# Linear attention, a mixture of experts and an MLP on one core: the mask table's source, the order of the input loads, and the last slot's routing

## The chip, the cores and the metric

The kernel runs on one core of one Trainium2 chip. A core has five engines that run their own instruction streams: PE (matrix products), DVE and POOL (elementwise work), ACT (activation functions, copies with a scale) and SP (which here only issues DMAs). DMAs are issued by SP, ACT and POOL and are carried out by 16 DMA engines. The metric is the device time of one launch in microseconds (us), the median of several runs.

## The reference

Three stages follow each other. First a linear attention with decay, for 2 batches, 8 heads, 768 positions and 64 dimensions per head:

```python
for b in range(nb):                                   # blocks of 64 positions
    intra = (q_b @ k_b.T * Dmask) @ v_b               # Dmask[i,j] = lam**(i-j) for i >= j, else 0
    inter = (q_b * lam**(pos+1)) @ kv_state
    out[b] = intra + inter
    kv_state = lam**block * kv_state + (k_b * lam**(block-1-pos)).T @ v_b
```

Its output, 1536 tokens of 512 numbers, goes through a mixture of 8 experts in which each token takes the one expert whose embedding is nearest to it: `out = gate * (relu(x @ w1[e]) @ w2[e])`, with 512 by 1024 and 1024 by 512 weights per expert. The result goes through an MLP with 2048 hidden units, `elu(x @ w_in) @ w_out`. The MLP's weights arrive as 64-bit floats and are converted on the chip.

## The kernel before

The kernel works in 12 **slots** of 128 tokens: slot s is block s // 2 (128 positions) of batch s % 2. A slot's input is 1 MB, loaded by two DMAs of 512 KB: `load_a` brings the queries and keys (lines 323 to 331), `load_b` the keys again in the other layout and the values. Everything is issued in an order written out by hand (`manual_schedule`), so each engine's stream is what the code says.

Attention per slot: `stage_a` forms the scores (PE, `st`, L344), `mask` multiplies them by the decay table `Dm` (DVE, `stm`, L352), `queries` and `keys` scale q and k (POOL, `qd` and `kd`), `stage_b` adds the state's part and the part inside the block (PE, `xp`, L380 and L387) and copies the sum to SBUF (ACT, `xs`), `products` and `add` update the state `S` (PE `kr` L407, POOL L412, DVE L422). `stage_c` is a generator whose steps are handed out one at a time: transpose and router logits (PE `tm`), logits to SBUF (DVE `lg`), the row's norm (ACT `sq`, `yr`; DVE `nrm`, `rs`), the token rows as a high half (ACT L449) and a low half (DVE L452) of 16-bit numbers, and the DMA `rows<-row` that writes them to DRAM (SP, L455). Between these steps `self.step()` hands out one piece of weight preparation: ACT L151 writes a weight's high half, DVE L155 the low half, and the freed buffer's next load (`raw<-w`, 1 MB, SP, L129) is issued.

The decay table. `powers` (L266) forms the powers of lam, one head in each of the partitions 0 to 7 (`zs`, 8 rows of 256 numbers: zeros, then 128 powers), and writes them to DRAM (`Z`, 8 KB, on ACT's queue). `masks` reads `Dm` (128 partitions by 8 heads by 128) back from `Z` by one DMA of 512 KB whose partition p starts p numbers further on, and `scales` reads `L`, the powers per head pair, by two DMAs of 128 KB; POOL then multiplies `L` by lam (L486).

Inputs. Slots 0 to 5 are loaded at the start. `IN_AT = {2: 6, 3: 7, 4: 8, 5: 9, 8: 10, 9: 11}` says at which slot's turn which further slot is loaded; slots 4 and 5 live in two of the six weight buffers of the attention phase (`IN_W`), the others in four input buffers.

DMA counters. Each DMA issued from SP or ACT signals one of eight counters, DMAHW0 to DMAHW7, taken in turn in the program's order over both queues; before a counter is taken again, the issuing engine waits until the DMA that had it eight issues before has landed. The names in the rows of order below are these counters.

The end of the attention. Slots 9, 10 and 11 don't go through DRAM for expert 0: `first_gather` fetches expert 0's rows among slots 0 to 8 by two indirect DMAs on POOL (`g<-rows,idx`, 128 and 96 rows, L762), and `dispatch` sums them and the rows of slots 9 to 11 into `px` by products on PE (L725 and L729 for the gathered rows, L712 for the slots), using one-hot matrices `oh` from `places`. `route` ranks the tokens of a slot within their expert (PE `kr<-M`, L631 and L634, then DVE). The program waits, before the first gather, for the index tile `idx` (DVE L677) and for the DMAs that wrote the rows of slots 0 to 8.

Lines 536 to 566 order all this by hand; `go(a, b, ...)` takes one step of each generator named. Then `moe_mlp` runs the experts (PE `ph` L942, `py` L981) and the MLP (`pf` L1023, `po` L1063).

Of the kernel before, what the change touches and what calls it, by code (L numbers as in the profile page):

```python
# [9 lines left out]
F32 = mybir.dt.float32  # L10
# [35 lines left out]

IN_W = (4, 5)
IN_AT = {2: 6, 3: 7, 4: 8, 5: 9, 8: 10, 9: 11}
ATT_LOADS = (2, 4, 5, 6, 7)
# [15 lines left out]
class K:  # L65
    def __init__(self, ctx, tc, A, out, dbg=None):
        self.ctx, self.tc, self.nc, self.A, self.out = ctx, tc, tc.nc, A, out
        self.dbg = dbg or {}
        self.raws = {}
        self.wts = {}  # L70
        self.next_load = 0
        self.ring = []
# [30 lines left out]
    def piece_scale(self, i):  # L103
        if i < 4 * E:
            return (S_W1, S_W2)[(i % 4) // 2]
        return (S_WI, S_WO)[(i - 4 * E) % 2]

    def w_free(self):

        n = len(self.ring)  # L110
        if len(self.wp) == 1:
            return n < WA
        return n < WA + WB or self.used.get(self.ring[n - WA - WB], self.group) < self.group

    def w_tile(self, i):
        self.ring.append(i)
        return self.wp[(len(self.ring) - 1) % (WA + WB) >= WA].tile([P, 2, 4, 512], F16, name=f"w{i}", tag="w")

# [147 lines left out]
    def powers(self, a1, ps):  # L266

        nc = self.nc

        Z = self.dp.tile([H, 256], F32, name="Z")  # L270
        zs = a1.tile([H, 256], F32, name="zs")
        nc.vector.memset(zs, 0.0)
        pw = a1.tile([P, H], F32, name="pw")
        nc.gpsimd.tensor_tensor(out=pw, in0=self.lam8, in1=self.pcol.to_broadcast([P, H]), op=ALU.pow)
        self.kdec = pw
        nc.tensor.matmul(ps[0:H, 0:P], pw, self.id32, start=True, stop=True, skip_group_check=True)
        nc.vector.tensor_copy(zs[:, 127:255], ps[0:H, 0:P])
        nc.scalar.dma_start(Z[:, :], zs)
        return Z[:, :]

    def masks(self, a1, zt):
        nc = self.nc
        self.Dm = a1.tile([P, H, P], F32, name="Dm")
        hank = bass.AP(tensor=zt.tensor, offset=zt.offset, ap=[[1, P], [256, H], [1, P]])
        nc.sync.dma_start(self.Dm, hank)

    def scales(self, a1, zt):

        nc = self.nc
        self.L = a1.tile([P, NP, P], F32, name="L")  # L290
        for hh in range(2):
            src = bass.AP(tensor=zt.tensor, offset=zt.offset + hh * 256 + 127, ap=[[0, 64], [512, NP], [1, P]])
            nc.sync.dma_start(self.L[hh * 64 : hh * 64 + 64], src)


    def attention(self, ctx):
# [171 lines left out]
        zt = self.powers(a1, ps_r)
        self.masks(a1, zt)
        load_a(2)  # L470
        load_b(2)
        self.scales(a1, zt)
        nc.scalar.dma_start(self.c32[:, 128:], A["c32"][:, 128:])
        for s in range(3, 6):
            load_a(s)
            load_b(s)
# [3 lines left out]
        for k in range(KD):  # L480
# [4 lines left out]
        keys(1)  # L485
        nc.gpsimd.tensor_tensor(  # L486
            out=self.L, in0=self.L, in1=self.lam4[:, :, None].to_broadcast([P, NP, P]), op=ALU.mult
        )
        stage_a(0)
# [8 lines left out]
        for s in range(1, FIRST + 1):  # L498
# [51 lines left out]
        stage_a(11)  # L550
        go(c8)
        self.step()
        go(c8, c9, r8, r8, c9, r8, c9, r8)
        stage_b(10)
        fg = self.first_gather(a1, ps_r)
        go(fg, c9, c9)
# [3 lines left out]
        go(t9, t9, t9, t9, c10, c10, c10)  # L560
        stage_b(11)
        go(c9, t10, t10, fg, c10, t10, fg, c10, t10)
        go(r10, r10, put, c10)
        go(c11, c11, t11, c11, t11, c11, t11, c11, t11)
        go(put, r11, c10, put, r11, put, c11, c11, put)
        go(r10, r10, r11, r11)
# [123 lines left out]
    def dispatch(self, a1, ps_s):  # L690
# [26 lines left out]
        places(FIRST, NS - 1)  # L717
        yield
        pts = [ps_s.tile([P, 2, 2, 256], F32, name=f"px{i}", tag="st") for i in range(2)]
        g0, g1 = self.G.pop((0, 0)), self.G.pop((0, 1))  # L720
        at = lambda k: pts[k // 4][:, k // 2 % 2, k % 2]
        for i in range(2):
# [9 lines left out]
            for s in range(FIRST, NS - 1):  # L732
                products(s, ks)
            if i == 0:
                yield
        yield
        places(NS - 1, NS)
        yield
        for b in range(2):
# [535 lines left out]
def layout(q, k, v, lam, moe_expert_emb, moe_tau, moe_w1, moe_w2, moe2_w_in, moe2_w_out):  # L1275
# [22 lines left out]
    wo = moe2_w_out.view(np.int64).reshape(4, 4, P, 512).transpose(0, 2, 1, 3)  # L1298
    c32, c16 = constants()
    i1 = np.tile(np.arange(1, CAP + 1, dtype=np.float32), (P, 1))  # L1300
    return dict(i1=i1, qkv=qkv, small=small, w1=w1, w2=w2, wi=wi, wo=wo, c32=c32, c16=c16)

# [16 lines left out]
```

## Time and profile before

| | us |
|---|---|
| median of 3 runs | 508.62 |
| lowest, highest run | 508.29, 512.58 |
| the profiled execution's own time | 509.62 |
| span from its first to its last instruction | 507.8 |

The profile is of one execution, so all places in time below are in us from the start of its span. Engines are busy: PE 471.9 (93%), DVE 347.1 (68%), ACT 224.4 (44%), POOL 77.1 (15%). A row of the timeline has the start, the duration, the engine, the line, the operation, output<-inputs, the shape, the count, and in brackets how long the engine stood idle before it and what ended that. SPq and ACTq are DMA issues. A row of the windows view has a stretch, its length, the busy time (and number) of PE, PE's weight loads, DVE, ACT and POOL, then the granted TensorE clock as a share of 2.4 GHz, the busy share of the DMA engines and the GB/s. "DMA to landing" is the time from a DMA's issue until it has landed.

The attention takes the first 80 us, the hand-over to expert 0 the next 12, the experts run to about 250 us and the MLP to the end.

### The profile page before, as it was taken

Reading aid. Unit: us, or ns where it says so; the run is one execution under the profiler, and the core shown is the slowest. Engines: PE = TensorE matmul, PEld = TensorE weight load, DVE = VectorE, ACT = ScalarE, POOL = GpSimd, SP = SyncE. Lnnn points to the kernel's source line nnn. Section 1 sums busy time; section 2 is a strip of 40 time slices with the busy share of each in tenths; the row PEclk is TensorE's granted clock in tenths of the full one; section 3 lists DMA queues with packets and bytes.
Section 4 is the critical chain, followed back from the end, with each engine's and each line's share of the span. In section 5 each row is a group of like instructions: output and inputs, shape, how many; then the busy total and the mean of one; then the engine's idle time right before and its main releaser. Section 6 shows DMA issues by size and latency. Waiting matters only on the chain.

```text
span 507.8 us, 9088 instructions
## 1 busy us (share of the span) xinstructions
PE 471.9 (93%) x3671; PEld 330.6 (65%) x3671; DVE 347.1 (68%) x625; ACT 224.4 (44%) x374; POOL 77.1 (15%) x67
## 2 busy tenths in 40 slices
PE   7788885998999999979999999999999999999992
PEld 6677775997999999979844444444444444445561
DVE  2467795466999988996878797978845335435352
ACT  1255344174686676423265354534333342433441
POOL 4456431351011310000000000000000002001111
PEclk9899898998999999999999999999999999999998
DMA  7999933267999999893622222000000001101101
GB/s 223 363 411 420 416 109 137 86 155 251 336 346 231 368 378 302 335 342 121 214 85 83 84 83 84 1 1 1 0 1 0 1 0 43 41 1 42 43 28 61
DMA packets 28335, 79.07 MB, mean 156 GB/s; under 512 B 13280, under 2 KB 15360, under 8 KB 22144
## 3 DMA queue, kind: packets, MB, share of 16 engines
q1 hardware_dynamic: 25848, 71.42, 41.4%
q0 software_dynamic: 2112, 6.82, 4.1%
q8 instruction: 31, 0.51, 0.4%
q10 hardware_dynamic: 328, 0.19, 0.1%
q14 instruction: 16, 0.13, 0.1%
HBM read 68.57 MB, written 7.10 MB: 149 GB/s over the span
## 4 chain that ended last, share of the span: by engine, by line
PE 77%; DVE 5%; DMA 3%; SPq 1%; issue 1%; ACT 1%; POOL 0%; POOLq 0%; DVEq 0%
PE pf L1023 25%; PE po L1063 24%; PE ph L942 14%; PE py L981 13%; DMA x<-g 2%; DVE w L155 1%; SPq L921 1%; DVE stm L352 1%; DMA g<-rows,idx 1%; PE px L712 1%; DMA out<-o,idx 1%; DVE S L422 0%; DVE row L452 0%; PE st L344 0%; PE pt L926 0%
## 5 line engine op out<-in xcount | busy, mean ns | idle before, releaser
L1023 PE MATMUL pf<-yT,w 128*128 128x512 f16 (+2 forms) x672 | 133.2, 349 | 0.0
L1063 PE MATMUL po<-w,g 128*128 128x512 f16 x576 | 133.1, 379 | 0.0
L1023 PEld LDWEIGHTS <-w 128*128 128x128 f16 x672 | 62.4, 98 | 65.4
L1063 PEld LDWEIGHTS <-g 128*128 128x128 f16 x576 | 55.9, 98 | 65.5 <-DVE g L1049 0.5
L1033 DVE TENSOR_TENSOR et<-pf,bc 128x512 f32<-128x512 f32 (+2 forms) x56 | 34.4, 614 | 91.5 <-PE pf L1023 91.4
L1034 ACT ACTIVATE eu<-et 128x512 f32<-128x512 f32 (+2 forms) x56 | 31.9, 569 | 140.0 <-DVE et L1033 140.0
L942 PE MATMUL ph<-x,w 128*128 128x224 f16 x768 | 75.2, 259 | 4.0 <-DMA x<-g 2.9
L981 PE MATMUL py<-h,w 128*128 128x224 f16 x768 | 76.6, 262 | 2.2 <-DVE w L155 2.2
L155 DVE SCALAR_TENSOR_TENSOR w<-raw,w 128x1024 f16<-128x1024 f32 x64 | 76.7, 1228 | 0.1
L981 PEld LDWEIGHTS <-w 128*128 128x128 f16 x768 | 74.2, 99 | 3.4 <-DVE w L155 2.4
L942 PEld LDWEIGHTS <-w 128*128 128x128 f16 x768 | 73.4, 98 | 4.7 <-DMA x<-g 3.1
L151 ACT ACTIVATE w<-raw 128x1024 f16<-128x1024 f32 x64 | 64.9, 1049 | 4.2 <-DVE cs L875 2.4
L1082 POOL DMA_INDIRECT out<-o,idx x12 | 11.8, 986 | 307.1 <-DVE o L1080 283.6
L762 POOL DMA_INDIRECT g<-rows,idx x16 | 22.1, 1383 | 84.3 <-DMA x<-g 58.8
L1049 DVE SCALAR_TENSOR_TENSOR g<-et,g 128x512 f16<-128x512 f32 (+2 forms) x56 | 34.1, 608 | 0.2 <-ACT g L1043 0.2
L1042 DVE SCALAR_TENSOR_TENSOR et<-eu,et 128x512 f32<-128x512 f32 (+2 forms) x56 | 33.9, 606 | 0.3 <-ACT eu L1035 0.3
L1035 ACT ACTIVATE eu<-eu 128x512 f32<-128x512 f32 (+2 forms) x56 | 31.9, 570 | 1.8
L1043 ACT ACTIVATE g<-et 128x512 f16<-128x512 f32 (+2 forms) x56 | 30.9, 553 | 0.3 <-DVE et L1042 0.3
L950 ACT ACTIVATE h<-ph 128x448 f16<-128x448 f32 x32 | 17.3, 541 | 21.4 <-PE ph L942 17.2
L951 DVE SCALAR_TENSOR_TENSOR h<-ph,h 128x448 f16<-128x448 f32 x32 | 19.8, 617 | 10.0 <-ACT h L950 9.9
L151 ACT ACTIVATE w<-cv 128x1024 f16<-128x1024 f32 x16 | 16.8, 1050 | 14.3 <-DVE cv L220 14.3
L987 ACT ACTIVATE yT<-py 128x448 f32 (+1 forms) x16 | 8.7, 545 | 32.2 <-PE py L981 32.2
(183 smaller groups left out, 403.4 us busy)
## 6 DMA issues: line engine op xcount, KB each, us to landing
raw<-w SPq DMA_DIRECT2D x32, 1024.0 KB, 7.9
in<-qkv SPq DMA_DIRECT2D x20, 512.0 KB, 7.6
raw<-wi SPq DMA_DIRECT2D x8, 1024.0 KB, 6.5
raw<-wo SPq DMA_DIRECT2D x8, 1024.0 KB, 7.9
rows<-row SPq DMA_DIRECT2D x15, 256.0 KB, 6.4
win<-qkv SPq DMA_DIRECT2D x4, 512.0 KB, 9.5
bc<-cd SPq DMA_DIRECT2D x1, 768.0 KB, 4.3
Dm<-Z SPq DMA_DIRECT2D x1, 512.0 KB, 3.9
```

The costliest lines, as they stand in the source:

```text
L151: nc.scalar.activation(out=o[0], in_=x, func=AF.Copy, scale=sc)
L155: nc.vector.scalar_tensor_tensor(out=o[1], in0=x, scalar=sc, in1=o[0], op0=ALU.mult, op1=ALU.subtract)
L942: nc.tensor.matmul(ps[:, j, :], w[:, wl, k, c : c + P], x[:, xl * KD + k, :], start=(n == 0), stop=(n == 11))
L981: nc.tensor.matmul(ps[:, j, :], w[:, wl, f % 4, c : c + P], h[:, hl, f, :], start=(n == 0), stop=(n == 23))
L1023: nc.tensor.matmul(ps[:, :n], w[:, wl, k, c : c + P], yT[yl][:, k, t0 : t0 + n], start=(i == 0), stop=(i == 11))
L1033: nc.vector.tensor_tensor(out=t[:, :n], in0=UT[m, f][:, :n], in1=self.bc[:, t0 : t0 + n], op=ALU.mult)
L1034: nc.scalar.activation(out=u[:, :n], in_=t[:, :n], func=AF.Relu, scale=-1.0)
L1035: nc.scalar.activation(out=u[:, :n], in_=u[:, :n], func=AF.Exp, scale=-1.0)
L1042: nc.vector.scalar_tensor_tensor(out=t, in0=u, scalar=-1.0, in1=t, op0=ALU.add, op1=ALU.max)
L1043: nc.scalar.activation(out=g[:, 0, :n], in_=t, func=AF.Copy, scale=S_G)
L1049: nc.vector.scalar_tensor_tensor(out=g[:, 1, :n], in0=t, scalar=S_G, in1=g[:, 0, :n], op0=ALU.mult, op1=ALU.subtract)
L1063: nc.tensor.matmul(acc[t], g[:, gl, t * P : t * P + P], w[:, wl, f % 4, :], start=(f == first and i == 0), stop=(f == last and i == 2),)
```

## The change

Three parts, and a ring of weight buffers that follows from the second.

1. **The table.** `Z` is gone. `Dm` is read straight from `zs` in SBUF, by eight DMAs of 64 KB, one for each head, alternately on ACT's and SP's queue. `L` is formed on PE from `zs` and a new constant `sel` (8 by 512, loaded on ACT's queue), and multiplied by lam on DVE instead of POOL. The input of slot 2 is no longer loaded between `masks` and `scales` but right after the table's DMAs.
2. **The inputs.** `IN_AT` is s + 4 for every s from 2 to 7: slots 10 and 11 are asked for at slots 6 and 7 instead of 8 and 9, and live in weight buffers. The ring of weight buffers is kept per pool, and a buffer may be used again within the attention once its user is finished.
3. **The last slots' order.** Slot 8's rows are finished (`c8` twice) before the piece of weight preparation instead of after it. `places` for slot 11, and the `route` ranking it needs, come ahead of the first products on the gathered rows.

```diff
-IN_W = (4, 5)
-IN_AT = {2: 6, 3: 7, 4: 8, 5: 9, 8: 10, 9: 11}
+IN_W = (4, 5, 10, 11)
+IN_AT = {s: s + 4 for s in range(2, 8)}
...
+    def w_slot(self):
+        for p, n in zip(range(len(self.wp)), (WA, WB)):
+            r = self.rings[p]
+            if len(r) < n or self.used.get(r[-n], self.group) < self.group:
+                return p
+        return None
...
-        Z = self.dp.tile([H, 256], F32, name="Z")
...
         nc.vector.tensor_copy(zs[:, 127:255], ps[0:H, 0:P])
-        nc.scalar.dma_start(Z[:, :], zs)
-        return Z[:, :]
...
+        for i, h in enumerate((0, 2, 4, 6, 1, 3, 5, 7)):
+            z = zs[h : h + 1, 0:P]
+            src = bass.AP(tensor=z.tensor, offset=z.offset, ap=[list(z.ap[0]), [1, P], [1, P]])
+            (nc.scalar, nc.sync)[i % 2].dma_start(self.Dm[:, h, :], src)
+        lp = self.ps_x.tile([P, NP, P], F32, name="lp", tag="xp")
+        for a in range(NP):
+            nc.tensor.matmul(
+                lp[:, a, :], self.sel[:, a, :], zs[:, 127:255], start=(a == 0), stop=True, skip_group_check=True
+            )
+        nc.vector.tensor_tensor(out=self.L, in0=lp, in1=self.lam4[:, :, None].to_broadcast([P, NP, P]), op=ALU.mult)
...
-        go(c8)
+        go(c8, c8)
         self.step()
-        go(c8, c9, r8, r8, c9, r8, c9, r8)
+        go(c9, r8, r8, c9, r8, c9, r8)
...
-        go(c11, c11, t11, c11, t11, c11, t11, c11, t11)
-        go(put, r11, c10, put, r11, put, c11, c11, put)
+        go(c11, c11, t11, c11, t11, t11, t11, r11, c10, r11, put, c11, c11, c11, put, c11, put, put)
...
         places(FIRST, NS - 1)
         yield
+        places(NS - 1, NS)
+        yield
```

**SP at the start of the program, before.** The DMAs for slots 0 and 1 stand ahead of these rows; `in_134` is slot 2's input, `in_141` slot 3's, `win_144` slot 4's.

```order
L285 DMA Dm<-Z 128x8x128 [waits DMAHW6_49,DMAHW0_49]
L330 DMA in_134<-qkv 128x1024 [waits DMAHW1_49]
L334 DMA in_134<-qkv 128x1024 [waits DMAHW2_49]
L293 DMA L<-Z 64x4x128 [waits DMAHW3_49]
L293 DMA L<-Z 64x4x128 [waits DMAHW4_49]
L330 DMA in_141<-qkv 128x1024 [waits DMAHW5_49]
```

**The same place now.** `in_149` is slot 2's input, `in_152` slot 3's. The counters 3 to 6 were last taken by the two halves of slot 0 and slot 1 (3 and 4, 5 and 6).

```order
L287 DMA Dm<-zs 128x1x128 [waits DMAHW0_49,DVE_49]
L287 DMA Dm<-zs 128x1x128 [waits DMAHW2_49]
L287 DMA Dm<-zs 128x1x128 [waits DMAHW4_49]
L287 DMA Dm<-zs 128x1x128 [waits DMAHW6_49]
L332 DMA in_149<-qkv 128x1024 [waits DMAHW0_49]
L336 DMA in_149<-qkv 128x1024 [waits DMAHW1_49]
L332 DMA in_152<-qkv 128x1024 [waits DMAHW2_49]
```

SP's four table DMAs are heads 2, 6, 3 and 7. The last of them waits for counter 6, the second half of slot 1's input, and slot 2's input stands behind it.

**DVE at slot 8's rows, before.** `row_831` is slot 8's row, `w_642` the low half of a weight.

```order
L422 TENSOR_TENSOR S_101<-S_101,kr 64x4x64 x2
L155 SCALAR_TENSOR_TENSOR w_642<-raw_422,w_642 128x1024
L452 SCALAR_TENSOR_TENSOR row_831<-tm_775,rs,row_831 128x512
L640 TENSOR_TENSOR t_854<-kr,M 128x24
L642 TENSOR_REDUCE r<-t_854 128x3
```

**The same place now** (`row_841` is slot 8's row).

```order
L424 TENSOR_TENSOR S_101<-S_101,kr 64x4x64 x2
L454 SCALAR_TENSOR_TENSOR row_841<-tm_785,rs,row_841 128x512
L160 SCALAR_TENSOR_TENSOR w_655<-raw_432,w_655 128x1024
L640 TENSOR_TENSOR t_864<-kr,M 128x24
L642 TENSOR_REDUCE r<-t_864 128x3
```

Slot 8's low half has changed places with a weight's. On SP the DMAs that follow them change places too: `rows<-row` of slot 8 now stands ahead of a `raw<-w` of 1 MB.

**DVE at slot 11's routing, before.** `M` is slot 11's chosen expert, `row_982` the low half of slot 10's row, `oh_978` slot 11's places, `row_1053` the low half of slot 11's row.

```order
L609 SCALAR_TENSOR_TENSOR sc_994<-lg,mx,c_81 128x8
L441 TENSOR_SCALAR nrm<-yr 128x1
L618 TENSOR_REDUCE m_177<-sc_994 128x1
L445 RECIPROCAL rs<-nrm 128x1
L620 TENSOR_TENSOR M<-sc_994,m_177 128x8
L452 SCALAR_TENSOR_TENSOR row_982<-tm_925,rs,row_982 128x512
L640 TENSOR_TENSOR t_1048<-kr,M 128x8
L642 TENSOR_REDUCE r<-t_1048 128x1
L700 SCALAR_TENSOR_TENSOR key<-r,M 128x1
L704 TENSOR_TENSOR oh_978<-iota_83,key 128x224
L452 SCALAR_TENSOR_TENSOR row_1053<-tm_984,rs,row_1053 128x512
```

**The same place now.**

```order
L609 SCALAR_TENSOR_TENSOR sc_1004<-lg,mx,c_81 128x8
L618 TENSOR_REDUCE m_188<-sc_1004 128x1
L620 TENSOR_TENSOR M<-sc_1004,m_188 128x8
L454 SCALAR_TENSOR_TENSOR row_992<-tm_935,rs,row_992 128x512
L640 TENSOR_TENSOR t_1022<-kr,M 128x8
L642 TENSOR_REDUCE r<-t_1022 128x1
L700 SCALAR_TENSOR_TENSOR key<-r,M 128x1
L704 TENSOR_TENSOR oh_988<-iota_83,key 128x224
L443 TENSOR_SCALAR nrm<-yr 128x1
L447 RECIPROCAL rs<-nrm 128x1
L454 SCALAR_TENSOR_TENSOR row_1029<-tm_994,rs,row_1029 128x512
```

Slot 11's norm (`nrm`, `rs`) went from ahead of its chosen expert to behind its places. On PE the twelve small products `kr<-M` for slot 11 (L631, L634) went from between the first and the second half of the `px` products to ahead of all of them.

## Rows read from the trace of the kernel before

**Rows 1.** The page: the span, and GB/s moved in 40 equal slices.

```profile
span 507.8 us, 9088 instructions
...
GB/s 223 363 411 420 416 109 137 86 155 251 336 346 231 368 378 302 335 342 121 214 85 83 84 83 84 1 1 1 0 1 0 1 0 43 41 1 42 43 28 61
```

**Rows 2.** Windows: a stretch of the MLP.

```profile
300.00:400.00 100.00, 100.00 (x465) 45.36 (x464) 69.91 (x96) 40.82 (x66) 0.00 (x0) 1.00 0.03 11
```

**Rows 3.** Timeline of the start: warm-up products, slot 1's keys, the table, slot 2.

```profile
5.60 2.93 PE L460 MATMUL kr<-ones 128*128 128x128 f32 x12 [0.37 <-DVE zs L277]
...
9.43 0.40 SPq L285 DMA_DIRECT2D Dm<-Z  x1
...
9.87 0.58 SPq L330 DMA_DIRECT2D in<-qkv  x1
...
10.32 1.04 POOL L358 TENSOR_TENSOR kd<-in,pw 128x512 f32<-128x512 f32 x1 [1.40 <-DMA in<-qkv]
...
13.43 1.29 DVE L352 TENSOR_TENSOR stm<-st,Dm 128x512 f32<-128x512 f32 x2 [1.57 <-DMA Dm<-Z]
...
15.62 2.01 PE L344 MATMUL st<-in 64*128 64x128 f32 x16 [4.15 <-DMA in<-qkv]
...
17.55 1.85 PE L387 MATMUL xp<-stm,in 128*64 128x128 f32 x16
```

**Rows 4.** Windows: the table's and slot 2's transfers; the stretch after slot 2's input came.

```profile
10.50:15.50 5.00, 0.96 (x24) 0.70 (x20) 3.32 (x7) 0.00 (x0) 0.87 (x1) 1.00 0.94 269
...
15.50:19.00 3.50, 3.38 (x30) 3.16 (x32) 1.29 (x2) 0.00 (x0) 0.59 (x1) 0.53 1.07 350
```

**Rows 5.** The page's DMA issues: engine, count, KB each, us to landing.

```profile
Dm<-Z SPq DMA_DIRECT2D x1, 512.0 KB, 3.9
```

**Rows 6.** Timeline: two masks in the middle; slot 11's input asked for, and used.

```profile
40.66 1.29 DVE L352 TENSOR_TENSOR stm<-st,Dm 128x512 f32<-128x512 f32 x2 [0.85 <-PE st L344]
...
46.16 1.29 DVE L352 TENSOR_TENSOR stm<-st,Dm 128x512 f32<-128x512 f32 x2 [0.85 <-PE st L344]
...
58.24 0.33 SPq L330 DMA_DIRECT2D in<-qkv  x1
...
70.06 1.16 PE L344 MATMUL st<-in 64*128 64x128 f32 x16
```

**Rows 7.** Timeline from slot 8's rows to the first gather.

```profile
72.06 1.23 DVE L155 SCALAR_TENSOR_TENSOR w<-raw,w 128x1024 f16<-128x1024 f32 x1
...
73.32 0.33 SPq L129 DMA_DIRECT2D raw<-w  x1
73.32 0.75 DVE L452 SCALAR_TENSOR_TENSOR row<-tm,rs,row 128x512 f16<-128x512 f32 x1
...
77.34 0.15 DVE L677 CAST idx<-kr 128x2 uint32<-128x2 f32 x1
...
81.47 1.18 POOL L762 DMA_INDIRECT g<-rows,idx  x1 [11.01 <-DVE M L620]
```

**Rows 8.** Line L455, all 15 writes of rows: us to landing.

```profile
DMA to landing us min/median/max: 2.1/6.4/7.7
```

**Rows 9.** Line L455 from 72 to 82 us, slot 8's alone.

```profile
L455 SPq DMA_DIRECT2D rows<-row x1: 616/616/616, 74.1 to 74.1; - x1
...
DMA to landing us min/median/max: 6.2/6.2/6.2
```

**Rows 10.** Timeline from slot 11's expert to expert 0's input.

```profile
84.23 0.15 DVE L620 TENSOR_TENSOR M<-sc,m 128x8 f16<-128x8 f32 x1
...
86.64 0.50 PE L729 MATMUL px<-idv,g 96*128 96x96 f16 x4 [1.01 <-DMA g<-rows,idx]
...
88.50 0.43 PE L634 MATMUL kr<-M,c 128*128 128x8 f16 x11
...
91.69 1.16 DVE L742 CAST x<-px 128x448 f16<-128x448 f32 x2 [1.07 <-PE px L712]
```

**Rows 11.** Windows: the products on the gathered rows.

```profile
84.00:90.50 6.50, 4.47 (x42) 3.74 (x43) 2.47 (x10) 0.69 (x1) 0.00 (x0) 0.50 0.35 132
```

More of the change, by code (lines that the diff above doesn't have):

```diff
@@ L71, in __init__ @@
         self.next_load = 0
-        self.ring = []
+        self.rings = [], []
         self.hold = False
@@ L106, in piece_scale @@
         return (S_WI, S_WO)[(i - 4 * E) % 2]
+    def w_slot(self):
[4 more added lines that the diff above has]
+        return None
     def w_free(self):
[L110 to L113, printed above, removed]
+        return self.w_slot() is not None
     def w_tile(self, i):
-        self.ring.append(i)
-        return self.wp[(len(self.ring) - 1) % (WA + WB) >= WA].tile([P, 2, 4, 512], F16, name=f"w{i}", tag="w")
+        p = self.w_slot()
+        self.rings[p].append(i)
+        return self.wp[p].tile([P, 2, 4, 512], F16, name=f"w{i}", tag="w")
     def load(self):
@@ L277, in powers @@
         nc.vector.tensor_copy(zs[:, 127:255], ps[0:H, 0:P])
-        nc.scalar.dma_start(Z[:, :], zs)
-        return Z[:, :]
-    def masks(self, a1, zt):
-        nc = self.nc
         self.Dm = a1.tile([P, H, P], F32, name="Dm")
[L284 to L289, printed above, removed]
+        for i, h in enumerate((0, 2, 4, 6, 1, 3, 5, 7)):
[7 more added lines that the diff above has]
+            )
         self.L = a1.tile([P, NP, P], F32, name="L")
-        for hh in range(2):
-            src = bass.AP(tensor=zt.tensor, offset=zt.offset + hh * 256 + 127, ap=[[0, 64], [512, NP], [1, P]])
-            nc.sync.dma_start(self.L[hh * 64 : hh * 64 + 64], src)
+        nc.vector.tensor_tensor(out=self.L, in0=lp, in1=self.lam4[:, :, None].to_broadcast([P, NP, P]), op=ALU.mult)
     def attention(self, ctx):
@@ L463, in attention @@
         nc.scalar.dma_start(self.id32, A["c32"][:, 0:128])
+        self.sel = a1.tile([H, NP, P], F32, name="sel")
+        nc.scalar.dma_start(self.sel, A["sel"])
         for s in range(2):
@@ L467, in attention @@
         warm(6)
[L468 to L472, printed above, removed]
+        self.powers(a1, ps_r)
         nc.scalar.dma_start(self.c32[:, 128:], A["c32"][:, 128:])
-        for s in range(3, 6):
+        for s in range(2, 6):
             load_a(s)
@@ L485, in attention @@
         keys(1)
-        nc.gpsimd.tensor_tensor(
-            out=self.L, in0=self.L, in1=self.lam4[:, :, None].to_broadcast([P, NP, P]), op=ALU.mult
-        )
         stage_a(0)
@@ L529, in attention @@
                 self.finished(f"in{s - 1}")
+            self.group += 1
             if s == 7:
@@ L733, in dispatch @@
                 products(s, ks)
[L734 to L738, printed above, removed]
+            yield
         for b in range(2):
@@ L1299, in layout @@
     c32, c16 = constants()
+    sel = np.zeros((H, NP, P), np.float32)
+    for h in range(H):
+        sel[h, h // 2, (h % 2) * 64 : (h % 2) * 64 + 64] = 1
     i1 = np.tile(np.arange(1, CAP + 1, dtype=np.float32), (P, 1))
-    return dict(i1=i1, qkv=qkv, small=small, w1=w1, w2=w2, wi=wi, wo=wo, c32=c32, c16=c16)
+    return dict(i1=i1, sel=sel, qkv=qkv, small=small, w1=w1, w2=w2, wi=wi, wo=wo, c32=c32, c16=c16)
 def kernel(**inputs):
```

2 lines of the change are left out of this document (added).

## Prediction

> **What bounds the kernel now.** I read the windows first. From about 120 us on PE has no gaps: in a stretch of 100 us of the MLP it is busy for all of them at the full 2.4 GHz [rows 2]. Nothing of the change touches a product there, and the order of the weight preparation on ACT and DVE stays as it was but for one swap, so everything behind the first product of expert 0 moves as one block. What the change can win or lose lies in the first 92 us of the 507.8 [rows 1].
>
> That stretch has three pieces, read from the timeline. *The start*: PE waits 4.15 us for slot 2's queries and keys, until 15.62 [rows 3]. The table, asked for at 9.43, lands 3.9 us later [rows 3, 5], and the first mask, idle for 1.57 us, begins at 13.43. But the first `xp` stands behind slot 2's scores on PE and starts only at 17.55 [rows 3]: the wait that ends last is slot 2's input, not the table. *The middle*: the masks of two neighbouring slots start at 40.66 and 46.16 [rows 6], 5.5 us apart, each after a wait for PE, which waits in turn for the state's sum on DVE. It is a chain of dependent work, no load holds it, so a shift at the start passes through to its end. *The hand-over*: the first gather starts at 81.47 [rows 7], its second part is used at 86.64 and expert 0's input is copied at 91.69 [rows 10], with PE at half rate (0.50) [rows 11].
>
> **The table and slot 2.** The transfer from `Z` cannot start before `Z` is written, which is why SP issues it at 9.43 and slot 2 at 9.87 [rows 3]. Now the table's first DMAs can go when `zs` is ready, at about 5.6, the time at which the warm-up products that wait for it start [rows 3]. This looks like a gain of nearly 4 us, but the counters take it back: SP's fourth table DMA needs the counter of slot 1's last half, whose landing starts POOL at 10.32 [rows 3], and slot 2 stands behind it in SP's queue. So SP issues that DMA at about 10.3 and slot 2 at about 10.8, later than the 9.87 of before. What is gained is that 64 KB stand directly ahead of slot 2 instead of 512. Before, 1 MB (table and half a slot) took from 9.43 to 15.62, 6.2 us: some 1.1 us until bytes flow at 10.5, then 269 GB/s [rows 4], thus 3.9 us, and 1.2 us to the end. With 576 KB: 1.1 + 2.2 + 1.2 = 4.5 us after 10.3, which is 14.8, a gain of 0.8 us. Against it, ACT's first three table DMAs (192 KB) now share the engines with slot 1's input; at 411 GB/s, the page's third slice [rows 1], they delay it by 0.5 us. Net: **-0.3 us**.
>
> This takes the read of the table from SBUF at the price of the nearest row, the same 1024 runs of 512 bytes out of DRAM, 3.9 us [rows 5]; no row shows a read of this size out of a few partitions. Below: free, and slot 2 comes a little earlier still; then PE's stretch at 0.53 of its clock (15.50 to 19.00 [rows 4]), in which 16 score products and 16 `xp` products take 3.9 us [rows 3], could go too, which is worth up to 1.9 us. So the lower end is -0.8 - 1.9 = -2.7 us. Above: if eight of 128 partitions gave only their share of 411 GB/s, 25.7, the table would take 20 us, about 12 us worse at slot 2. I take the row, since the runs and the destination are the same.
>
> The other edits of the start are costed at nothing. Four products for `L` are some eight records at 0.24 us (2.93 for 12 [rows 3]), 2.0 us on PE ahead of the warm-up; the router's constants on DVE come up to 2 us later, and on ACT a table load waits behind a DMA that needs slot 1's first half. They may push the first mask from 13.43 to 13.8 or so; the cover is PE's wait for slot 2, behind which `xp` stands anyway. Without that cover they cost 0.4 us. DVE pays 0.65 us for `L` (half of the 1.29 of two masks [rows 3]); POOL is freed of the same product, which no row shows on the path.
>
> **Inputs four slots ahead: 0.** Slot 11 is asked for at 58.24 and used at 70.06 with no wait [rows 6]; asking earlier shortens nothing. It moves 2 MB into a stretch where the slices already stand at 411 to 420 GB/s [rows 1], so rows and weights there come up to 5 us later. Rows are overwritten only three slots (16 us) on and land within 7.7 [rows 8]. If a weight came too late for ACT, each us would move the chain by one: bound +2.
>
> **The hand-over.** The gather needs `idx`, done at 77.49, and slot 8's rows [rows 7]. Those are issued at 74.1, behind 1 MB of weights asked for at 73.32, and land 6.2 us later, at 80.3 [rows 7, 9]; the DVE instruction that the row names as releaser isn't among what the gather waits for. Now the low half comes 1.23 us earlier, at 72.1, its DMA at 72.9, with the weights behind it. Landing then takes between 2.1 and 6.2 us [rows 8, 9]: 75.0 to 79.1. `idx` is late next, at 77.5. Between landing and start lay 1.2 us (80.3 to 81.47), so the gather starts at 78.7, 2.8 us earlier, and its second part is usable at 86.64 - 2.8 = 83.8.
>
> Then PE is not free for it: slot 11's ranking stands ahead of the products and needs slot 11's expert, made at 84.23 [rows 10]. Two small DVE operations that waited for ACT now come after it, so I put it at 83.8; twelve products of 0.43 us [rows 10] follow, and `px` starts at 84.3 with all gathered rows there. Before, from 86.64 to 91.69 PE worked 5.05 us [rows 10] for the rest of `px` and that ranking; without 0.43, and with the four products done before 86.64 (as long as the 0.50 of the other four), it is 5.1 us: 84.3 + 5.1 = 89.4. The norm of slot 11 that is moved back costs two small operations on DVE and half a row on ACT and DVE (0.7 each), ready near 87.5, needed near 88.5: covered; without cover up to 1 us. **-2.2 us.** Ends: the gather starts as before and only the ranking's 0.43 is won (-0.4); or PE keeps its full clock because it idles less, and the products that now lie in a half-rate stretch [rows 11] take half (-3.3).
>
> **Sum.** The profiled execution took 509.62, 1.82 more than its span; the median of the runs is 1.0 lower, 508.62. -0.3 - 2.2 = -2.5: 507.1 for a profiled execution, **506.1** for the median. The parts add, as the middle passes a shift on.
>
> **Rivals.**
>
> *A, slower: the table's read is slow at its source.* The eight heads lie in partitions 0 to 7, two groups of four. If each group answers at a sixteenth of the rate seen, 25.7 GB/s, 512 KB take 10.2 us. From 6.7 (issue at 5.6, 1.1 us until bytes flow) that is 16.9; before, slot 2 came 2.3 us after the table (13.3 to 15.62), now at 19.2: +3.6 us, and the hand-over's -2.2 leaves +1.4, 510.0. It decides once the table takes over 8.5 us, where the loss at the start eats the hand-over's gain. For it: all reads go to eight partitions, and slot 2 is queued behind them. Against: no row shows such a limit. [...]
>
> *B: the hand-over wins nothing.* PE is at half rate in the whole stretch, or the gather is held by something not seen in the 1.2 us before its start: -0.3 - 0.4 gives 507.9.
>
> *C: both ends go well.* -2.7 and -3.3: 502.6.
>
> **Chances.** Forecast 0.42; A 0.30, as a mechanism that fits the change but has no row; B 0.14; C 0.14. Of C most lies more than 1% faster (under 503.5), of A a little more than 1% slower (over 513.7, the proportional share above); 1% is about what a measurement of this kernel can tell from no change. Faster 0.12, same 0.81, slower 0.07. The range holds the forecast, B, most of A and half of C: 503.2 to 510.6; the forecast's own is 504.5 to 507.5.
>
> **What would show it.** Right: SP's last table DMA at 10 to 11 us; the last of the table by 13.5; slot 2's scores near 15.3; slot periods of 5.5 us; slot 8's rows landed before 77.5, the gather near 78.7; PE waiting for slot 11's expert, not for the gather; `x` copied 2.5 us earlier than 91.69. Wrong: a table that lands at 17 or later (A); `px` waiting for the gather or at 0.50 throughout (B); a new wait in the middle for a weight or an input; a gap behind 120 us that is not there now.

## The result, and the profile after

The changed kernel takes **514.66 us** (median; 511.94 to 520.24) beside 509.17 us for the kernel before: a ratio of 1.0109, 95% interval 1.0084 to 1.0133. It is slower by 5.5 us where 2.5 us less were forecast. The ratio leaves out one execution of the changed kernel, the 520.24 us, which lies over 1.5% above its fastest. Its profiled execution took 515.12 us.

The page of the changed kernel: the span, GB/s in 40 equal slices, and the table's DMAs on SP's queue (count, KB each, us to landing).

```profile
span 513.3 us, 9122 instructions
...
GB/s 190 179 392 382 421 295 124 80 137 290 325 321 262 392 359 315 334 299 155 213 86 82 83 82 84 0 1 1 0 1 0 1 0 56 27 2 62 22 42 45
...
Dm<-zs SPq DMA_DIRECT2D x4, 64.0 KB, 10.6
```

The second slice (12.8 to 25.7 us) moves 179 GB/s where before it moved 363 [rows 1], and 64 KB out of SBUF take 10.6 us to land where 512 KB out of DRAM took 3.9 [rows 5]. The timeline of the start says what that did (the ACT_TABLE_LOAD row stands right ahead of ACT's first work on the router's constants):

```profile
5.06 0.28 DVE L281 COPY zs<-kr 8x128 f32<-8x128 f32 x1 [3.94 <-PE kr L280]
5.36 8.45 SPq L287 DMA_DIRECT2D Dm<-zs  x4
5.37 8.48 ACTq L287 DMA_DIRECT2D Dm<-zs  x4
...
13.86 2.58 SPq L332 DMA_DIRECT2D in<-qkv  x1
...
13.88 2.59 ACTq L473 DMA_DIRECT2D c<-c  x1
...
16.51 1.28 ACT L580 ACT_TABLE_LOAD   x1 [16.51 <-DMA Dm<-zs]
...
19.80 0.69 DVE L354 TENSOR_TENSOR stm<-st,Dm 128x512 f32<-128x512 f32 x1
20.90 0.69 DVE L354 TENSOR_TENSOR stm<-st,Dm 128x512 f32<-128x512 f32 x1 [0.40 <-DMA Dm<-zs]
...
23.19 1.23 PE L346 MATMUL st<-in 64*128 64x128 f32 x8 [9.29 <-DMA in<-qkv]
```

The table is asked for at 5.36 and is all in only just before 20.90, where the second half of the first mask waits for it. SP and ACT need 8.5 us to issue four DMAs each, waits for counters included, and slot 2 goes out at 13.86. Its scores start at 23.19, after PE has waited 9.29 us; before it was 15.62 after 4.15 [rows 3]. That is 7.6 us lost. ACT, which now issues half of the table, comes to its table load at 16.51 instead of 6.54, and the last of the router's constants is ready only at 19.78, right ahead of the first half of the mask. The transfer rate in the stretch is in the windows of the changed kernel (PE, its weight loads, DVE, ACT, POOL, then granted clock, DMA share and GB/s):

```profile
9.00:17.00 8.00, 4.90 (x57) 4.57 (x55) 0.19 (x1) 0.49 (x1) 1.04 (x1) 1.00 0.67 49
```

From 9 to 17 us little but the table moves, at 49 GB/s, while the DMA engines are busy for 0.67 of the time. Before that the inputs of slots 0 and 1 fill them, at 406 GB/s from 7 to 8 us.

The hand-over, from slot 8's rows to expert 0's input:

```profile
80.48 0.75 DVE L454 SCALAR_TENSOR_TENSOR row<-tm,rs,row 128x512 f16<-128x512 f32 x1
85.64 0.15 DVE L677 CAST idx<-kr 128x2 uint32<-128x2 f32 x1
...
86.09 1.88 POOL L760 DMA_INDIRECT g<-rows,idx  x1 [7.21 <-DVE idx L677]
...
92.28 0.17 PE L631 MATMUL kr<-M,c 128*128 128x8 f16 x1 [1.13 <-DVE M L620]
...
97.99 1.16 DVE L740 CAST x<-px 128x448 f16<-128x448 f32 x2 [2.43 <-PE px L712]
```

The gather starts 0.3 us after the index tile is done, where it started 4.0 after it [rows 7], PE waits for slot 11's expert and not for the gather, and from the start of the `idx` row to the copy of `x` it is 12.35 us instead of 91.69 - 77.34 = 14.35 [rows 7, 10]. So expert 0's input is copied 6.3 us later than before: 8.3 from the start, less 2.0. (The 2.0 are those of this one pair of profiles; the pairs of kernels in the next section show less.)

Behind that, the shift does not stay the same. First the kernel before, then the changed one: expert 0's second layer, the last expert's first layer, the last products.

```profile
117.19 9.12 PE L981 MATMUL py<-h,w 128*128 128x224 f16 x76 [2.19 <-DVE w L155]
...
222.06 9.36 PE L942 MATMUL ph<-x,w 128*128 128x224 f16 x96 [2.90 <-DMA x<-g]
...
495.96 2.90 PE L1063 MATMUL po<-w,g 128*128 128x512 f16 x12
```

```profile
122.64 7.46 PE L979 MATMUL py<-h,w 128*128 128x224 f16 x76 [2.19 <-DVE w L160]
...
224.91 9.36 PE L940 MATMUL ph<-x,w 128*128 128x224 f16 x96 [2.02 <-DMA x<-g]
...
498.81 2.90 PE L1061 MATMUL po<-w,g 128*128 128x512 f16 x12
```

The 76 products take 9.12 us in one execution and 7.46 in the other: in the first a part ran at half rate (granted clock 0.86 from 118 to 130 us, 0.50 from 119 to 121), in the second at full rate, after the same idle time of 2.19 us. The last expert's wait for its transposed rows is 2.02 instead of 2.90. So the last products are only 2.85 us late. Behind them come 8.9 us to the end of the span before, and 11.6 after. A tail and a half-rate stretch can differ between two executions of one kernel: e12 and e13 below are one kernel with tails of 9.3 and 11.5 us, e4 and e7 one kernel whose last expert's first layer takes 11.02 us (granted clock 0.84) and 9.36 (1.00). So the 5.5 us of the two spans is not one sum of steps; the medians say 5.5 as well. Whether these 76 products too would differ from one execution of a kernel to the next isn't shown.

### The profile page after: what moved, and what is told of

The parts are those of the page before. It is cut to its first block, busy times and chain, and to the rows that moved or that the text cites. A ratio compares the mean times of both kernels' runs of the same rounds, so it can differ in the third digit from the quotient of the medians.

```text
span 513.3 us, 9122 instructions
## 1 busy us (share of the span) xinstructions
PE 474.2 (92%) x3679; PEld 333.8 (65%) x3679; DVE 347.3 (68%) x626; ACT 224.8 (44%) x374; POOL 74.9 (15%) x66
## 4 chain that ended last, share of the span: by engine, by line
PE 79%; DMA 10%; DVE 5%; SPq 2%; ACT 1%; issue 1%; POOL 0%; POOLq 0%; DVEq 0%
PE pf L1021 24%; PE po L1061 24%; PE ph L940 14%; PE py L979 12%; DMA in<-qkv 5%; DMA win<-qkv 2%; DMA rows<-row 1%; DMA x<-g 1%; SPq L287 1%; PE tm L431 1%; DVE w L160 1%; SPq L919 1%; PE px L712 1%; DVE row L454 1%; PE st L346 1%; DVE stm L354 1%
## 5 line engine op out<-in xcount | busy, mean ns | idle before, releaser
L979 PE MATMUL py<-h,w 128*128 128x224 f16 x768 | 74.9, 259 | 2.2 <-DVE w L160 2.2
L760 POOL DMA_INDIRECT g<-rows,idx x16 | 20.7, 1296 | 79.8 <-DMA x<-g 57.2
L156 ACT ACTIVATE w<-cv 128x1024 f16<-128x1024 f32 x16 | 16.8, 1051 | 14.5 <-DVE cv L225 14.5
## 6 DMA issues: line engine op xcount, KB each, us to landing
win<-qkv SPq DMA_DIRECT2D x8, 512.0 KB, 11.6
Dm<-zs SPq DMA_DIRECT2D x4, 64.0 KB, 10.6
```

The lines of the kernel that those rows point to most:

```text
L156: nc.scalar.activation(out=o[0], in_=x, func=AF.Copy, scale=sc)
L979: nc.tensor.matmul(ps[:, j, :], w[:, wl, f % 4, c : c + P], h[:, hl, f, :], start=(n == 0), stop=(n == 23))
```

## The experiments

The theory: the table's read is limited where it is read from, in eight partitions that it takes for two groups of four; this costs the start some 7 us, and the hand-over gives about 2 back. Its rivals: the loss lies in the number of DMAs and their counters, or in parts 2 and 3. Ratios are to the kernel before, timed beside each kernel.

| kernel | ratio (95% interval) | slot 2's scores start, us | idx to copy of x, us |
|---|---|---|---|
| before | 1 | 15.62 | 14.35 |
| changed | 1.0109 (1.0084 to 1.0133) | 23.19 | 12.35 |
| e1: part 1 alone | 1.018 (1.0136 to 1.0224) | 23.04 | 12.81 |
| e2: part 3 alone | 0.997 (0.9939 to 1.0) | 15.73 | 12.66 |
| e9: part 2 alone | 1.0012 (0.9981 to 1.0043) | 15.64 | 12.62 |
| e3: parts 2 and 3 | 0.9965 (0.9934 to 0.9995) | 15.83 | 12.32 |
| e4: changed, heads in partitions 0, 4 to 28 | 0.9995 (0.9964 to 1.0025) | 17.49 | 11.49 |
| e8: e3, slot 2 ahead of the table | 0.9981 (0.995 to 1.0013) | no wait | 11.56 |
| e11: table by eight DMAs from DRAM, slot 2 ahead | 0.9978 (0.995 to 1.0007) | no wait | 12.27 |
| e13: e8, first weight a slot later | 0.9912 (0.9873 to 0.9951) | no wait | 11.91 |

**The three parts apart.** e1 takes part 1 (the table and `L`) into the kernel before, e2 part 3 (the order of the last slots and `places`), e9 part 2 (`IN_AT`, `IN_W` and the ring), e3 parts 2 and 3 together.

> The kernel before with part 1 alone (the table read from SBUF, L on PE). In the changed kernel's trace slot 2's scores start at 23.19 us instead of 15.62, 7.6 us later, while its median is 5.5 us over the kernel before, 514.66 against 509.17. Theory: the start costs 7.6 us and the hand-over of part 3 gives 2 us of it back, so this kernel is the slowest: slot 2's scores near 23, about 7.5 us over the kernel before, 516.7. Rival: something in parts 2 and 3 makes the loss too (late weights, a longer tail, which is 11.6 us behind the last product instead of 8.9): then this kernel is at 514.7 or below it, although its start is as late.

Part 1 alone is the slowest of the timed kernels: 519.2 us beside 509.8, 9.2 us more by the ratio where 7.5 were expected. Its start is that of the changed kernel:

```profile
23.04 2.08 PE L341 MATMUL st<-in 64*128 64x128 f32 x16 [9.00 <-DMA in<-qkv]
```

> The kernel before with part 3 alone (the order of the last slots). Theory: gather 3 to 4 us earlier after the index tile than before, expert 0's input copied 2 us earlier (near 89.7 instead of 91.69), and nothing of it given back behind it: 507.1, 2.0 us under the kernel before. Rival: the 2 us are given back before the end of the experts, as the changed kernel's shift shrinks from 6.3 us at expert 0 to 2.85 us at the MLP: then within 0.7 us of the kernel before.

508.13 beside 509.79, a gain of 1.5 us, between 3.1 and nothing: the interval holds the theory's 2.0 and the rival's 0.7. The copy of `x` was expected near 89.7 and starts at 90.92, 0.77 us earlier than before. Two other pairs that differ by part 3 show no more: 89.96 in e3 against 90.85 in e9, and 97.99 in the changed kernel against 98.44 in e1, where part 2 differs too.

> The changed kernel with part 1 undone (the table through DRAM, L by DMA and POOL, as before), so parts 2 and 3 alone. Theory: part 2 costs nothing and the start is that of before (slot 2's scores at 15.6), so the same as part 3 alone: 507.1, between 506 and 508. Rival: part 2 costs something of its own, by late rows or weights or at the end: 508.5 or more, and slower than part 3 alone by over 1 us.

508.16, a gain of 1.8 us (0.25 to 3.4). Against the changed kernel the ratio is 1.0109 / 0.9965 = 1.0145: part 1 costs 7.4 us when it is added to the others (5.4 to 9.4 when the two intervals are put together), 9.2 alone (6.9 to 11.4). Both hold the 7.6 us of the start; parts 2 and 3 cost nothing.

> The kernel before with part 2 alone (inputs four slots ahead, the ring of weight buffers per pool). Theory: it costs and gives nothing, 509.7 like the kernel before, within 1 us; the masks of slots 3 to 9 start within 0.4 us of before. Rival: inputs asked for earlier delay the first weights, which ACT waits for already (1.18 us instead of 0.68 near 32 in the kernel without part 1): then the masks from slot 6 on start 0.3 to 0.5 us later and the time is 0.5 to 1 us longer.

511.3 beside 511.69 in that set of runs: no difference that can be measured, though the masks from the third on start 0.6 to 0.7 us later up to 50 us, more than the 0.4 expected. The rival isn't excluded at its own size of half a microsecond.

**Where the table is read from.** e4 puts head h into partition 4h, by a product whose weights have the powers in every fourth column, and e5 into partitions 0 to 3 and 32 to 35; the number of DMAs, the bytes, the order and the queues stay. In e4

```diff
-            z = zs[h : h + 1, 0:P]
+            z = zs[4 * h : 4 * h + 1, 0:P]
```

and in e5

```diff
-            z = zs[h : h + 1, 0:P]
+            r = h % 4 + 32 * (h // 4)
+            z = zs[r : r + 1, 0:P]
```

> The changed kernel with one head of the table in each of the partitions 0, 4, 8 to 28 instead of 0 to 7 (the same eight DMAs in the same order, the same bytes and runs). Source theory: in the changed kernel's trace the DMA engines move 44 to 63 GB/s from 9 to 17 us, while the table is read out of two groups of four partitions, about 24 GB/s for each. Eight groups then give about 190 GB/s: 512 KB in 2.7 us, the table all in by 13.5, SP's last table DMA near 10, slot 2's scores near 15, and the time of parts 2 and 3 alone, 507 (506 to 508.5). Rival, number of DMAs: what is slow is eight DMAs of 128 runs of 512 bytes, each held by a counter, wherever they read from: then nothing changes, slot 2's scores stay near 23 and the time near 514.7. [...]

> The changed kernel with the heads of the table in partitions 0 to 3 and 32 to 35, eight partitions again (same eight DMAs). What sets the pace of the read is open in two ways. If it is the number of partitions read from, or each DMA by itself, nothing changes: slot 2's scores start near 23 as in the changed kernel, the time stays near 514.7. If partitions 32 to 35 answer through the same door as 0 to 3, only one door of about 24 GB/s is left (44 to 63 GB/s were seen with partitions 0 to 7): 512 KB take some 21 us, of which about a seventh is moved beside the inputs before 9 us, so the last of the table lands near 29 and slot 2's scores start at 31 to 33, the time near 523. [...]

Landing of the eight table DMAs, by their issuing line, in the changed kernel, then e4, then e5:

```profile
DMA to landing us min/median/max: 7.8/9.3/10.9
```

```profile
DMA to landing us min/median/max: 5.0/5.1/5.6
```

```profile
DMA to landing us min/median/max: 9.5/15.5/18.4
```

And e5's windows and slot 2's scores:

```profile
10.00:22.00 12.00, 2.59 (x46) 2.33 (x44) 0.00 (x0) 0.00 (x0) 1.04 (x1) 0.78 0.66 25
```

```profile
30.11 2.08 PE L351 MATMUL st<-in 64*128 64x128 f32 x16 [17.52 <-DMA in<-qkv]
```

The number of partitions is eight each time. Out of 0 to 3 with 32 to 35, one group in the theory, the read goes at 25 GB/s, out of 0 to 7, two groups, at 49, which is 24.5 for each; and e5's one run takes 521.35 us, near the 523 expected (its scores start 1 us earlier than expected). So it is which partitions are read that sets the rate here, not how many: partitions 32 to 35 beside 0 to 3 gave no more than 25 GB/s, 4 to 7 beside them gave 49.

In e4 the read is no longer the bottleneck that it was, and 5.8 of the 7.4 us come back (1.0109 against 0.9995; 3.8 to 7.8), but slot 2's scores start at 17.49, not at 15. One head's DMA still takes 5 us to land, the last one goes out when a counter of slot 1's input is free, at 10.0, and slot 2 stands behind it: from 10 to 13 us only 104 GB/s move.

```profile
10.00:13.00 3.00, 2.30 (x40) 2.04 (x38) 0.12 (x1) 1.65 (x4) 1.06 (x1) 0.88 0.77 104
```

```profile
17.49 2.08 PE L350 MATMUL st<-in 64*128 64x128 f32 x16 [5.18 <-DMA in<-qkv]
```

**The number of DMAs.** e6 writes the table to DRAM as before and reads it by the same eight DMAs.

```diff
+        nc.scalar.dma_start(Z[:, :], zs)
...
-            src = bass.AP(tensor=z.tensor, offset=z.offset, ap=[list(z.ap[0]), [1, P], [1, P]])
+            src = bass.AP(tensor=zt.tensor, offset=zt.offset + 256 * h, ap=[[1, P], [1, P]])
```

> The changed kernel with the table written to DRAM again as before and read from there by the same eight DMAs of 64 KB, in the same order on the same two queues. Source theory: each lands some 4 us after its issue, the write of the 8 KB is through at 9.4 as before, so the table is in by about 14; slot 2 then waits for a counter of one of these DMAs (13.4) and its scores start at 17 to 18, the time near 510. Rival, number of DMAs and counters: the table stays as slow as from SBUF, over 7.8 us from issue to landing, slot 2's scores at 23 or later, 514.7 or more.

```profile
DMA to landing us min/median/max: 2.9/3.0/3.0
```

```profile
17.53 1.16 PE L348 MATMUL st<-in 64*128 64x128 f32 x16 [3.42 <-DMA in<-qkv]
```

Each lands in 3.0 us instead of 9.3, and slot 2 comes at 17.53, as the source theory had it; eight DMAs as such aren't slow. The one run took 506.06 us, less than the 510 expected but inside the 505.7 to 512.63 that the kernel before spans in the same set, so it decides nothing on the time.

**What is late besides slot 2.** e10 asks for slot 2's first half ahead of the slow table.

```diff
+        load_a(2)
         self.powers(a1, ps_r)
...
-        for s in range(2, 6):
+        load_b(2)
+        for s in range(3, 6):
```

> The changed kernel (table from partitions 0 to 7) with the first half of slot 2's input asked for ahead of the table's DMAs. Theory: slot 2 was late only because it stood behind the slow table, on SP's queue and on the counters; now its scores start by 12.5, and what is late is the table alone: the first mask at 20 to 21 as in the changed kernel, the first sum inside the block near 22 instead of 25.3, the time 511 to 512.5. Rival: the slow read holds up every other transfer beside it: slot 2's scores still start after 20 and nothing is won, 514.7.

```profile
13.12 1.16 PE L346 MATMUL st<-in 64*128 64x128 f32 x16
...
14.78 2.97 ACTq L474 DMA_DIRECT2D c<-c  x1
...
17.78 1.28 ACT L582 ACT_TABLE_LOAD   x1 [17.78 <-DMA Dm<-zs]
...
20.87 0.19 DVE L484 TENSOR_TENSOR ie<-small,es 128x32 f32<-128x32 f32 x1
21.08 1.29 DVE L354 TENSOR_TENSOR stm<-st,Dm 128x512 f32<-128x512 f32 x2
21.82 2.35 PE L389 MATMUL xp<-stm,in 128*64 128x128 f32 x15 [7.54 <-DVE stm L354]
```

Slot 2's scores need no wait any more, the first sum starts at 21.82 (25.2 in the changed kernel, 17.55 before [rows 3]), and the 513.49 us of its one run are 1.8 over the median before of that set, not quite the 511 to 512.5 expected. So in these traces some 3.4 us of the 7.6 were slot 2 behind the table. What holds the first mask now is the chain of router constants: the row of ACT's table load names a table DMA, but ACT was issuing DMAs, four of the table and one of constants, until 17.75, and the last router constant is done right ahead of the mask. Slot 2's first half, queued ahead of the slow read, came in time.

**A start without the slow read.** e8 is e3 with `load_a(2)` ahead of `powers`; e11 is e6 with the edit of e10. (In the expectation of e12 the masks are counted from one: its "slot 6" is slot 5 here.)

> Parts 2 and 3 with the table through DRAM, and the first half of slot 2's input asked for ahead of the table's read on SP's queue (behind slot 1's input) instead of behind it. Theory: slot 2's queries and keys (512 KB behind slot 1's last half, which lands near 10.3) are in by 11.7, so that their scores no longer wait; the table, asked for at 9.4 and read in 3.9 us, is late next: first mask at 13.5, router constants no later, first sum inside the block near 15 instead of 17.0, and the time 2 us under parts 2 and 3 alone, 506.1. Rival: the table's read is delayed by what stands ahead of it (9.4 to landing over 6 us) and all is as before: 508.2.

508.35 beside 509.66: the first sum starts at 14.74 instead of 16.97 in e3, as expected, and nothing of it is seen in the time. The timeline of e8 shows where 1.1 us went; the kernel before comes first.

```profile
29.73 1.28 DVE L352 TENSOR_TENSOR stm<-st,Dm 128x512 f32<-128x512 f32 x2
...
32.73 1.06 ACT L151 ACTIVATE w<-raw 128x1024 f16<-128x1024 f32 x1 [0.68 <-DMA raw<-w]
...
35.16 1.29 DVE L352 TENSOR_TENSOR stm<-st,Dm 128x512 f32<-128x512 f32 x2
```

```profile
14.74 0.43 PE L392 MATMUL xp<-stm,in 128*64 128x128 f32 x2 [2.44 <-DVE stm L357]
...
27.92 1.28 DVE L357 TENSOR_TENSOR stm<-st,Dm 128x512 f32<-128x512 f32 x2
...
32.10 1.06 ACT L156 ACTIVATE w<-raw 128x1024 f16<-128x1024 f32 x1 [1.85 <-DMA raw<-w]
...
33.64 0.59 ACT L397 ACTIVATE xs<-xp 128x512 f32<-128x512 f32 x1
...
34.44 1.28 DVE L357 TENSOR_TENSOR stm<-st,Dm 128x512 f32<-128x512 f32 x2
```

ACT waits 1.85 us for the first weight's data, the copy of slot 3's output stands behind it on ACT, and slot 5's mask comes 6.52 us after slot 4's instead of 35.16 - 29.73 = 5.43 in the kernel before, where the same wait was 0.68. This is not all of it: the profiled execution of e8 took 505.0 us, the shortest of its twelve, and its last products are 4.5 us earlier than in the kernel before. Why the median shows less of it, no trace says.

> Parts 2 and 3, the table through DRAM read by eight DMAs on two queues, L on PE, and the first half of slot 2's input ahead of the table's read. Theory: the table lands 3 us after its issue at 9.6 to 11, its last head after slot 2's first half has freed its counter (11.7), thus at 14.7: first mask at 14.5 to 15, first sum inside the block near 15.8; what is won at the start beyond 0.7 us is taken back by ACT's wait for the first weight near 32, so about the same as with one DMA, 507.5 to 508.5. Rival: the one look at the eight DMAs from DRAM, 506.06, was no chance, since POOL no longer multiplies L: 506 or less.

509.91 beside 511.69, 1.1 us less by the ratio: within the theory, and no gain like that of e6's 506. The first mask was at 16.94 and not at 14.5 to 15, the first sum at 17.68 and not at 15.8; the mask stands right behind the router constants again, which ACT's table load starts at 13.63, behind ACT's own issues of table and constants.

> The table through DRAM and slot 2's first half ahead of it (as in the run that expected 506.1 and had 508.35), with the first piece of weight preparation one slot later, at slot 5 instead of 4 (one piece fewer is prepared in the attention). In that run ACT waited 1.85 us at 30.2 to 32.1 for the first weight's data, with the copy of slot 3's output behind it, and the mask of slot 6 came 6.52 us after that of slot 5 instead of 5.43. Theory: that wait took back the start's gain; now slot 6 follows slot 5 by 4.1 to 5.0 us, and its mask starts at 32.5 to 33.4 instead of 34.44. Rival: slot 6's own input (asked for near 20) holds it: still 34.4.

```diff
-ATT_STEPS = range(4, 10)
+ATT_STEPS = range(5, 10)
```

```profile
28.07 1.28 DVE L357 TENSOR_TENSOR stm<-st,Dm 128x512 f32<-128x512 f32 x2
...
33.52 1.29 DVE L357 TENSOR_TENSOR stm<-st,Dm 128x512 f32<-128x512 f32 x2 [1.19 <-PE st L349]
...
218.39 10.66 PE L948 MATMUL ph<-x,w 128*128 128x224 f16 x96 [4.96 <-DMA x<-g]
```

The mask starts at 33.52, 5.45 us after the one ahead of it: the 1.1 us are back, so the wait for the first weight had taken them, though the spacing was expected even shorter. The copy of `x` comes 5.8 us earlier than before (85.91), but the last expert's wait for its rows grows from 2.90 to 4.96, and one run took 507.64.

> The same kernel as in the look before (table through DRAM, slot 2's first half ahead of it, first weight one slot later, parts 2 and 3), now timed. Theory: expert 0 starts 5 to 6 us earlier than before, but the last expert's input waits for its transposing DMA, behind 4 MB of weights on SP's queue, until about 218, so that 2 to 3.5 us are left at the end: a ratio of 0.993 to 0.996 to the kernel before. Rival, the shift passes through: 5.8 us, a ratio of 0.989.

505.69 beside 509.6, a ratio of 0.9912 (0.9873 to 0.9951): faster than both kernels, by 4.5 us than the one before. In this profile the last expert's wait is 2.89 us again (216.14) and the last products are 5.9 us earlier than before, so of the two theories the point lies between, and the interval holds the rival and most of the theory's range. Against e8 the ratios differ by 3.5 us (1.0 to 6.1). In the traces slot 11's mask is 1.9 us earlier than in e8: 1.1 come at the first weight's wait, and 1.4 between the masks of slots 8 and 9, where PE's granted clock is 1.00 from 51 to 60 us and was 0.81 in e8, less 0.6 for a later start. But the edit also leaves one piece of preparation fewer to the attention, and e6, without the edit, has 1.00 there too; so how much of the 3.5 us is the first weight's place alone isn't shown.

**The tail.** e7 is e4's kernel once more (its label says slot 2 first, its code doesn't).

> A second look at the kernel of the eight groups (heads in partitions 0, 4 to 28). Its first look had a tail of 11.6 us behind the last product where the kernel with the table through DRAM had 8.7. If the tail is set by chance from run to run, it is between 8.7 and 9.7 in about half of the looks; if it belongs to this kernel, it is 11.6 again. Slot 2's scores at 17.5 again, 1.9 us later than before.

Slot 2's scores started at 17.07, and the tail was 509.4 - 494.52 - 2.90 = 12.0 us, so it looked like a property of this kernel. But the kernel of e12 and e13 had 9.3 and 11.5, so one kernel can have either. Over all profiles the table from SBUF has 9.7 (e1, e5) to 12.0 us and the table from DRAM 8.7 to 10.0 but for e13's 11.5: that a part of the tail goes with the change isn't excluded. It is longer where the last scatters (`out<-o,idx`) take longer to land: 2.7 to 3.0 us in the kernel before, up to 4.6 in the changed one and 4.9 in e13. What sets that stays open.

## Why the prediction was wrong

**The start: the step that failed.** The prediction took "the read of the table from SBUF at the price of the nearest row", the read out of DRAM, because runs and destination were the same [rows 5]. The source was what mattered: 49 GB/s out of partitions 0 to 7, and 25 out of 0 to 3 with 32 to 35 (e5). The term was -0.3 us and measured +7.6 (e1, e3: 7.4 to 9.2 in the time).

**Rival A had the mechanism, with too small a price.** Its 51.4 GB/s is the 49 seen. No row stood behind its groups of four or the sixteenth for each: they were a supposition, and e5, at 25 GB/s where 25.7 was put for one group, is the run that bears it out. Its read began at 6.7; in the trace the DMA engines carry the inputs of slots 0 and 1 almost until 9, and 512 KB at 49 GB/s take 10.7 us from there, and with the 1.2 us that the prediction put at the end of a transfer that is 20.9: the table was in by 20.90. That this fits so well is in part luck: the table's packets start at 8.1, with 48 KB moved by 9 us, and go at about half that rate from 17 to their end at 20.4. Its 2.3 us from table to slot 2 came out right (23.19). With 9 us in place of 6.7 and 49 in place of 51.4 rival A would have read +7.6 at the start, and 514.0 in all. Its chance of 0.30 was too low for a mechanism that fits the change and that no row contradicts. Two of its figures don't follow from its own sum: for a table at 25.7 GB/s that gives 13.8 us at slot 2 instead of the "about 12" (e5, at 25, lost 14.5), and a loss that eats the hand-over's gain from 8.8 us of table on instead of 8.5.

**The counters.** SP's last table DMA was put at 10.3 and began at 9.8; that step held. What wasn't expected is that an issue itself lasted up to 4.0 us on SP with slow reads ahead of it (0.33 to 0.43 for the same DMAs out of DRAM, e6), so slot 2 went out at 13.86 instead of 10.8.

**Costs at nothing.** `lp` on PE (2.07 us), `L` on DVE (0.69) and POOL's relief cost nothing that the runs show. The router constants behind ACT's table load do cost something once slot 2 is less late: they hold the first mask in e4 (14.63, against 13.43 before [rows 3]), e6 (16.32), e10 (21.08) and e11 (16.94). The prediction named the cover, PE's wait for slot 2, and priced its loss at 0.4 us; with a table that is read fast (e4, e6, e11) the mask starts 1.2 to 3.5 us later. It saw ACT's table load behind a DMA and the constants up to 2 us later; that ACT issues half of the table itself, ahead of that load, moved the load from 6.54 to 11.34 in e4 and 16.51 in the changed kernel.

**"The middle passes a shift on."** For a loss it held: slots 5 and 6 of the changed kernel are 8.4 us late, slot 11 8.3, with spacings of 5.5. For a gain it failed: e8 lost 1.1 us of 1.8 at the first weight's wait. "Everything behind the first product of expert 0 moves as one block" was wrong in both directions: a half-rate stretch that costs 1.7 us is there in one execution and not in the other (9.12 against 7.46 us for the same 76 products), and the last expert's wait for its rows was 2.0 to 5.0 us.

**Inputs four slots ahead: 0.** Measured at -1.0 to +2.2 us (e9), so inside the bound. Rows did land later, after up to 12.0 us in e9 instead of 7.7 [rows 8]; the spacing of the masks does not show it.

**The hand-over: -2.2.** Each step was seen as put down: rows landed before `idx`, the gather right behind it, PE waiting for slot 11's expert. The size is less sure than the one trace made it: 14.35 us from `idx` to `x` is the longest of the kernels without part 3 (e1 and e9 had 12.81 and 12.62, with the gather 2.6 and 2.9 us behind the end of `idx`, not 4.0), and with it 11.5 to 12.7 were seen. The term was thus taken from an execution in which this stretch was 1.5 us longer than in the other two; the copy of `x` itself came only 0.45 to 0.89 us earlier in the three pairs of profiles above. Timed, part 3 is worth 1.5 us, between 0 and 3.1, which doesn't exclude 2.2. PE did not keep its full clock there, the case of the -3.3: it was at 0.50 from 91 to 97 us, as from 84 to 90 before.

## What to carry to other kernels

Look at a DMA's source as well as at its destination: the same eight DMAs with the same destination landed in 9.3 us out of partitions 0 to 7, in 5.1 out of 0, 4 to 28 (e4) and in 15.5 out of 0 to 3 with 32 to 35 (e5). When a table is read many times out of a few partitions, try other partitions, and compare with a bounce through DRAM, whose eight DMAs landed three times as fast here (3.0 us against 9.3), though they could only be asked for once the 8 KB were written (at 9.6 instead of 5.4). What was queued behind the slow transfer, on the queue, on its counter, and on the engine that issues it, paid as well (slot 2's scores 7.6 us later, ACT's table load 10.0); put what is needed first ahead of it. A gain at the front must be followed to the end for the next load that is asked for at a fixed place, here the first weight: with an edit there the gain of e8 that wasn't seen became 4.5 us over the kernel before, though the traces give only 1.1 us of it to that wait.

## What the runs showed of the hardware

- The DMA read rate out of eight partitions was 25 GB/s when they were 0 to 3 and 32 to 35 (e5), and 49 GB/s when they were 0 to 7 (changed kernel; 50 in e1). The same 64 KB DMA landed (median of eight) in 3.0 us out of DRAM (e6), 5.1 out of partitions 0, 4 to 28 (e4), 9.3 out of 0 to 7 and 15.5 out of 0 to 3 and 32 to 35.
- The DMA engines' busy share was 0.66 at 25 GB/s (e5, 10 to 22 us), 0.67 at 49 (changed kernel, 9 to 17 us) and 0.94 at 269 [rows 4].
- A DMA issue on SP, 0.40 and 0.58 us in [rows 3], lasted 2.58 us for slot 2 in the changed kernel and 5.28 in e5, behind slow reads.
- In the kernel before, PE's granted clock went to 0.50 at 15.73, 56.69, 84.00 and 118.13 us, in the changed one at 18.87, 66.66 and 90.55, and nowhere else in the first 130 us: each time inside an idle time of PE of 1.9 to 9.3 us or at most 1.2 us behind its end. But it stayed at 1.00 behind the 2.19 us up to 122.64 in the changed kernel, and in e4 it was 0.50 from 8 to 10 us with no idle time of PE above 0.61 us since 2.63. That PE keeps its full clock when it idles less is thus not shown.
- At granted clock 1.00, 465 products of 512 columns fill 100 us [rows 2], 2.38 columns per ns, an estimate of the full clock if a column takes a cycle; the prediction's 2.4 GHz stands on no view beyond this.
